# Second taps of the fourth group and their transfers ahead of the second group's result copies; fifth x, w2's sums and some scalings later; PSUM banks of one group dealt anew

## The chip, the core and the metric

The kernel runs on one core of a Trainium2 chip. A core has a matrix engine (TensorE, in the profile PE, with its weight loads as PEld), a vector engine (VectorE, DVE), a scalar engine (ScalarE, ACT), GpSimd (POOL), a sync engine that only issues transfers (SyncE, SP), and 16 DMA engines. Each engine works through its own list of instructions in order; semaphores tie the lists together. The metric is device time in microseconds (us) of one execution; less is better. The time before is 958.31 us, the median of three runs (956.83 to 960.3).

## The reference

Two blocks follow each other on x of 8 x 4224 x 192 in float32. First a causal convolution along the sequence, with 7 taps per head (8 heads of 24 columns), the taps softmaxed; then a layer norm without bias, an MLP 192 -> 768 -> 192 with relu, and a residual:

```python
w = softmax(weight)                       # [8, 7]
x_pad = concat([zeros(B, 6, D), x], 1)
y[b, s, h*24:(h+1)*24] = sum_k w[h, k] * x_pad[b, s + k, h*24:(h+1)*24]
mu, var = y.mean(-1), ((y - mu) ** 2).mean(-1)
yn = (y - mu) / sqrt(var + 1e-6) * g_ln
out = y + maximum(yn @ w_ch1, 0) @ w_ch2
```

## The kernel before, in words

**Groups.** The sequence is cut into 18 groups, g = 0 to 17, counted from zero in the code ("the fourth group" is g = 3, "the fifth x" is `xg[4]`). A group holds up to 16 rows of 192 columns for each of 128 partitions; group 0 has 6, group 1 has 8, groups 2 to 16 have 16, group 17 has 10. For each group x is loaded (`load_x`), convolved to `y`, transposed in 32 x 32 blocks to `yt` (DVE), taken up through w1 to the hidden tile `room` with relu, and taken down through w2 to `ot`; at last y is in `out` (`store_y`), and `ot` times the row's 1/std is added there by an accumulating DMA (`add_to_out`). The mean is folded into w1 and relu lets 1/std be applied behind w2, which is why the scaling (`scale`, L937 on ACT) comes last. 1/std is worked out by `root`, a chain of 19 small POOL instructions in two parts (9 before its first `yield`, 10 after), for two groups at a time; `next(pending, None)` in `up_mixed` puts each part in its place in the program.

**The convolution** is dealt out: tap 0 on ACT (`first_tap`, L375, into y), tap 1 on ACT (`second_tap`, L383, into a tile `tb`), and for g > 2 `tb` is added to y by four accumulating DMAs issued by POOL (`add_in_parts`, L408). Taps 2 to 6 are DVE instructions (`conv`, L416), one for each tap and head. For group 2 the third tap is on ACT too.

**Stages.** Groups 0 and 1 go through w1 and w2 by plain products (`up`, `down`). In `up(1)` six blocks f = 0..5 of 128 hidden columns are made, each into a set of four PSUM banks that ACT empties (L512); the two sets take turns, and `between` puts other ACT work behind an eviction. In `down(1)` PE makes two rows at a time into one bank (L799), ACT copies each bank out (L809), and second taps of group 3 stand behind the copies.
Groups 2 to 16 use a Strassen-Winograd scheme with seven products. `up_mixed(g)` does this in two passes, over hidden blocks 2 and 0..1 of each half (`one`, `two`), with two bank sets X and Y in turn: `evict` copies a set to SBUF on ACT (L637); `close` adds a set to an earlier partial result, either on DVE (L643) or by an ACT copy and an accumulating DMA issued by POOL (L601). Some of those copies lie for a while in parts of the tile that pass `two` writes later: `two.c22[:, 0:1]` is the source of the transfer that closes `one.c21`, and pass `two` evicts into the same place.
`down_fast(g, work)` does w2 the same way (PE at L854, ACT copies at L860, DVE sums at L897), with six banks. `work` is a list of ACT jobs (relus, scalings of the group before, first and second taps of group g + 2) that are put behind the copies, three, two, two and three behind each product's column blocks. Sums of w1's and w2's quarters (`w1sums`, `w2sums`, L573 on POOL) are made once, in group 1.

**What sets the order.** The order is written by hand: each engine runs its instructions in the order of the program text, and each wait holds all that is behind it on that engine. POOL's list holds its arithmetic and the issues of all accumulating transfers; SP's list holds the loads of x and the stores of y. Banks come from `take_bank` (one after the other, mod 8) and `take_set` (the next aligned four). `take_set` in `up_mixed` gives X, then Y; in `up_last`, for the last group, it gives Y, then X, while X is used first in both.

**Names and lines that matter here.** `between` L535-542; `up_mixed` L603-727 with `act_scales` L657 (two calls, L691 and L697), `store_y(g, nc.gpsimd)` L690, `work` L724-727; `down` L801-813; `down_fast` L835-913 with the bank deal L845-847; the main loop L1015-1078 with `load_x(g + 2)` L1018, `fourth_sum()` L1057, w2's sums L1058-1061, `pending = root(0)` L1062. The line `if g + 2 < NG and g != 1: load_x(g + 2)` loads x4 at the top of group 2. A load with `gate=True` puts a one-element DVE memset into the tile first, so that the transfer waits for that memset's place in DVE's list.

Of the kernel before, what the change touches and what calls it, by code (L numbers as in the profile page):

```python
# [16 lines left out]
def kernel(  # L17
# [29 lines left out]
    nc = tc.nc  # L47
    PSUM = bass.MemoryType.PSUM
    B, S, D = x.shape
    H, K = weight.shape  # L50
# [315 lines left out]
    def first_tap(g, heads=(0, H)):  # L366
        n = groups[g][2]
        if g == 1:

            y[g] = y[0][:, groups[0][2] :]  # L370
        elif heads[0] == 0:
            y[g] = ypool.tile([P, J, D], F32, tag="y", name=f"y{g}")
        for h in range(*heads):
            cs = slice(h * GRP, h * GRP + GRP)
            nc.scalar.mul(y[g][:, 0:n, cs], xg[g][:, 0:n, cs], taps[:, h, 0:1])  # L375
# [9 lines left out]
    def second_tap(g, heads=(0, H)):  # L385

        if heads[0] == 0 and g == 2:
            tb[g] = room[:, NF * J * Q :][:, 0 : J * D].rearrange("p (j d) -> p j d", d=D)
        elif heads[0] == 0:
            tb[g] = bpool.tile([P, J, D], F32, tag="tb", name=f"tb{g}")  # L390
        tap_products(g, tb[g], 1, heads)
        if g > 2 and heads[1] == H:
            add_in_parts(g, y[g], tb[g])
# [91 lines left out]
    def store_y(g, queue=nc.sync):  # L485
        n = groups[g][2]
        for ps, rows in rows_of_out(g, 0, n):
            queue.dma_start(out=rows, in_=y[g][ps, 0:n].rearrange("p j d -> p (j d)"))
# [46 lines left out]

    def between(g, f):

        if g == 1 and f == 4:
            first_tap(3, heads=(0, 3))
        elif g == 1 and f == 5:  # L540
            first_tap(3, heads=(3, H))
            second_tap(3, heads=(0, 2))

    def up(g):

# [57 lines left out]
    def up_mixed(g, ahead, pending):  # L603
# [53 lines left out]
        def act_scales(j1, j2):  # L657
            scale(before, j1, j2)
# [27 lines left out]
        p.product(X, a12, p.b21)  # L686
        for f in range(PAIR):
            p.close(p.c11[:, f : f + 1], X, rooms[0][:, f : f + 1], f)
        if g == 2:
            store_y(g, nc.gpsimd)  # L690
        act_scales(0, 1)  # L691
        p.product(Y, s2, p.t[0], False, False)
        p.evict(Y, p.c21)
        one.relu(one.c11)
        p.product(X, s3, p.t[1], True, False)
        p.evict(X, p.c22)
        act_scales(1, 2)  # L697
        p.product(Y, s1, p.b12, False, False)
        conv(g + 1, 2, 5)
        conv(g + 1, 5, 6, heads=(0, H // 2))  # L700
        p.close(p.c22, Y, rooms[1][:, 0:PAIR])
        p.product(X, a22, p.t[2], False)
        for f in range(PAIR):
            p.relu(p.c11[:, f : f + 1])
        lower_sum(g, (PAIR,))
        conv(g + 1, 5, 6, heads=(H // 2, H - 1))
        p.close(p.c21, X)
        p.product(Y, s4, p.b22, False)
        p.evict(Y, p.c12, True)
# [12 lines left out]
                    add_to_out(k, mid, n)  # L722

        work = [lambda: one.relu(one.c22)]  # L724
        work += [lambda j=j: scale_one(j) for j in range(2, done)]
        half = [lambda i=i: two.relu(two.c22[:, i : i + 1]) for i in range(PAIR)]
        return work[0:7] + [half[0], lambda: None, half[1]] + work[7:]

# [72 lines left out]
    def down(g):  # L801


        ot = out_tile(g)
        for j in range(0, groups[g][2], 2):
            bank = take_bank()[:, 0 : 2 * D].rearrange("p (j d) -> p j d", d=D)
            for i in range(2):
                down_row(bank[:, i], lambda f: ht[g][:, f, j + i].rearrange("p q t -> p (q t)"))
            nc.scalar.copy(ot[:, j : j + 2, :], bank)  # L809
            if g == 0 and j:  # L810
                third_tap(2, (0, 4) if j == 2 else (4, H))
            elif g == 1 and j < 6:
                second_tap(3, heads=[(2, 4), (4, 6), (6, H)][j // 2])

    def quarters_of_w2():
        return [
# [18 lines left out]
    def down_fast(g, work):  # L835
        n = fast[g]
        t = width(g)
        w = n * T
        a = of_products(g)
        flat = cpool.tile([P, NC, NFAST * C], F32, tag="cs", name=f"cs{g}")[:, :, 0 : n * C]  # L840
        halves = "p c (h j t) -> p c h j t" if t == C else "p c (j h t) -> p c h j t"
        cs = flat.rearrange(halves, h=2, t=t)
        free = a[:, 1, 0].rearrange("p f q j t -> p (f q) j t")
        parts = [free[:, 0:CH], free[:, CH : 2 * CH]]
        banks = [take_bank() for c in range(CH) for i in range(2)]  # L845
        if g + 1 == NG:
            banks = [banks[CH * i + c] for c in range(CH) for i in range(2)]

        def product(bank, left, right, to, first, behind=0):
            for c in range(CH):  # L850
                dst = banks[2 * c + bank]
                for f in (PAIR, *range(PAIR)):
                    for q in range(NQ):
                        nc.tensor.matmul(  # L854
                            dst[C * q : C * q + C, 0:w], right[:, f, C * c : C * c + C],
                            left[:, f, q], start=(first and f == PAIR), stop=(f == PAIR - 1),
                            skip_group_check=True,
                        )
                if to is not None:
                    nc.scalar.copy(  # L860
                        to[:, c], dst[:, 0:w].rearrange("p (j t) -> p j t", t=t)
                    )
                for one in work[:behind]:
                    one()
                del work[:behind]

        b = quarters_of_w2()
        c11, c21 = cs[:, 0:CH, 0], cs[:, 0:CH, 1]
        c12, c22 = cs[:, CH:NC, 0], cs[:, CH:NC, 1]
        if g + 2 < NG:  # L870
            work += [
                lambda tap=tap, h=h: tap(g + 2, heads=(h, h + 1))
                for tap in (first_tap, second_tap) for h in range(H)
            ]
        behind = (3, 2, 2, 3) if g + 1 < NG else (0, 0, 1, 1)
        product(0, a[:, 0, 0], b[0], c11, True, behind[0])
        product(1, a[:, 1, 0], w2sums[:, 2], c22, True, behind[1])
        product(1, a[:, 1, 1], w2sums[:, 3], c21, False, behind[2])
        product(1, a[:, 0, 1], b[2], None, True, behind[3])
        if g + 1 < NG:  # L880
            transpose(g + 1)
        inner, upper, right = a[:, 1, 1], a[:, 0, 0], a[:, 0, 1]
        if g + 1 == NG:
            size = FC * NQ * w
            other = bpool.tile([P, J, D], F32, tag="tb", name="sums").rearrange("p j d -> p (j d)")
            inner, upper, right = [
                v.rearrange("p (f q j t) -> p f q j t", f=FC, q=NQ, t=t)
                for v in (other[:, 0:size], other[:, size : 2 * size], room[:, 0:size])
            ]
        order = (PAIR, *range(PAIR)) if g + 1 == NG else range(FC)  # L890
        for dst, left, right_of, op in (
            (inner, a[:, 1, 1], a[:, 1, 0], ALU.add),
            (upper, inner, a[:, 0, 0], ALU.add),
            (right, a[:, 0, 1], inner, ALU.subtract),
        ):
            for f in order:
                nc.vector.tensor_tensor(dst[:, f], left[:, f], right_of[:, f], op=op)  # L897
        for c in range(CH):
            nc.vector.tensor_tensor(
                c11[:, c], c11[:, c], banks[2 * c + 1][:, 0:w].rearrange("p (j t) -> p j t", t=t),  # L900
                op=ALU.add,
            )
        product(0, inner, w2sums[:, 1], parts[0], False, 2)
        product(0, upper, w2sums[:, 0], parts[1], False, 2)
        for one in work:
            one()
        product(0, right, b[3], c12, False)
        if g + 1 < NG:
            sums_of_y(g + 1, nc.gpsimd)()
            moments(g + 1)  # L910
        else:
            finish_fast(g, 0, flat, cs, parts)
        return flat, cs, parts
# [100 lines left out]
    b11, b12, b21, b22 = quarters_of_w2()  # L1014
    for g in range(NG):  # L1015
        last = g + 1 == NG
        if g + 2 < NG and g != 1:
            load_x(g + 2)  # L1018
        if g < 2:
            up(g)  # L1020
# [25 lines left out]
        if g == 1:  # L1046
            conv(2, 3)
            flat = [v.rearrange("p j d -> p (j d)") for v in (y[2], tb[2])]
            nc.vector.tensor_tensor(flat[0], *flat, op=ALU.add)
            let_in(w1sums[:, 2])  # L1050
            sums_of_quarters(w1sums[:, 2], w21, w1sums[:, 0])
            transpose(2)
            fourth_sum = sums_of_y(2, nc.gpsimd)
            nc.vector.tensor_tensor(w12, w12, w11, op=ALU.subtract)
            moments(2)
            down(g)
            fourth_sum()  # L1057
            sums_of_quarters(w2sums[:, 2], b12, b22)  # L1058
            sums_of_quarters(w2sums[:, 0], b12, b11)
            sums_of_quarters(w2sums[:, 1], b22, w2sums[:, 0])  # L1060
            sums_of_quarters(w2sums[:, 3], b21, w2sums[:, 1])
            pending = root(0)  # L1062
            continue
        if g + 2 < NG:
# [44 lines left out]
```

## Time and profile before

| what | us |
|---|---|
| time of the profiled execution | 958.28 |
| its span, first to last instruction | 956.4 |
| median of three runs | 958.31 |
| PE busy | 940.8 |
| DVE busy | 892.3 |
| ACT busy | 716.6 |
| POOL busy | 340.6 |

The granted TensorE clock is 0.999. PE is idle for some 15 us in all, and these idle stretches are few. The groups in the middle are alike: PE takes 27.61 us for `up_mixed` and 27.33 us for `down_fast` in most of them. Group 2 does not: its `up_mixed` runs from 80.22 to 113.51 (33.29 us) and its `down_fast` from 113.51 to 141.57 (28.06 us). Group 16's `down_fast` runs from 885.18 to 913.08 (27.90 us). In a timeline each row has the start and length in us, then engine, line, operation, what it writes and reads, the count, and in brackets the engine's idle time just before it and what ended it.

### The profile page before, as it was taken

The numbers are of one execution on the slowest core, as the hardware profiler recorded it, in microseconds if no ns is written. First come the engines' busy times: TensorE is split into PE (matmuls) and PEld (weight loads), VectorE is DVE, ScalarE is ACT, GpSimd is POOL, SyncE is SP. The second block draws the span as 40 slices with busy tenths as digits, with TensorE's granted clock in tenths as the row PEclk, the third lists the DMA queues.
The fourth block names the chain that finished last, engine by engine and source line by source line (L and its number), as shares of the span: only waits on it lengthen the run. The fifth ranks groups of instructions, "written<-read, shape, count | busy, mean of one in ns | idle before, by whom it ended". The sixth has DMA issues, their size and how long they took to land. (4 is left out here: it accounts for less than half of the span.)

```text
span 956.4 us, 38496 instructions
## 1 busy us (share of the span) xinstructions
PE 940.8 (98%) x17106; PEld 742.7 (78%) x17106; DVE 892.3 (93%) x1479; ACT 716.6 (75%) x1275; POOL 340.6 (36%) x463
## 2 busy tenths in 40 slices
PE   9999799999999999999999999999999999999997
PEld 7999659687786979677686968778696877869586
DVE  8996999999999999999999999999999999997885
ACT  7865678969687796968778795978789596867543
POOL 2037455141533227141443217231451415332140
PEclk9999999999999999999999999999999999999999
DMA  8396896988979797897978887896979889676631
GB/s 208 122 196 170 202 270 121 252 161 188 217 131 277 133 252 151 216 204 136 263 144 239 169 226 156 175 249 135 265 137 245 163 181 202 127 171 124 101 64 49
DMA packets 38347, 171.94 MB, mean 180 GB/s; under 512 B 4517, under 2 KB 5798, under 8 KB 32039
## 3 DMA queue, kind: packets, MB, share of 16 engines
q0 software_dynamic: 31488, 106.87, 60.3%
q1 hardware_dynamic: 6688, 62.61, 18.1%
q8 instruction: 134, 2.20, 0.9%
q14 instruction: 31, 0.25, 0.1%
q10 hardware_dynamic: 6, 0.00, 0.0%
HBM read 38.92 MB, written 50.92 MB: 94 GB/s over the span
## 5 line engine op out<-in xcount | busy, mean ns | idle before, releaser
L416 DVE SCALAR_TENSOR_TENSOR y<-xg,taps,y 128x384 f32<-128x384 f32 (+3 forms) x710 | 358.8, 580 | 11.3 <-issue 9.7
L854 PE MATMUL ps<-room,w2sums 128*32 128x256 f32 (+1 forms) x4464 | 244.1, 376 | 1.3 <-issue 1.3
L637 ACT COPY room<-ps 128x512 f32<-128x512 f32 (+1 forms) x225 | 180.5, 844 | 64.8 <-PE ps L522 61.9
L522 PE MATMUL ps<-yt,w 32*128 32x256 f32 (+3 forms) x4092 | 226.3, 365 | 1.6 <-ACT room L512 1.0
L854 PEld LDWEIGHTS ps<-room,w2sums 128*32 128x32 f32 x4464 | 146.4, 110 | 93.1 <-issue 2.4
L522 PEld LDWEIGHTS ps<-yt,w 32*128 32x128 f32 x4092 | 203.2, 185 | 19.6 <-issue 7.2
L854 PE MATMUL ps<-room,w 128*32 128x256 f32 (+1 forms) x3456 | 191.0, 373 | 1.7 <-DVE room L643 1.2
L897 DVE TENSOR_TENSOR room<-room 128x1024 f32<-128x1024 f32 x135 | 154.6, 1218 | 16.8 <-PE ps L854 14.0
L854 PEld LDWEIGHTS ps<-room,w 128*32 128x32 f32 x3456 | 111.6, 110 | 72.8 <-DVE room L643 6.4
L522 PE MATMUL ps<-ysums,w1sums 32*128 32x256 f32 (+1 forms) x2304 | 132.2, 371 | 0.0
L522 PEld LDWEIGHTS ps<-ysums,w1sums 32*128 32x128 f32 x2304 | 121.3, 185 | 5.3 <-issue 0.2
L948 POOL DMA_DIRECT2D out_dram<-ot x70 | 59.9, 986 | 180.5 <-ACT ot L937 175.2
L860 ACT COPY cs<-ps 128x256 f32<-128x256 f32 (+1 forms) x192 | 70.6, 368 | 47.5 <-PE ps L854 47.1
L937 ACT ACTIVATE ot<-ot,r 128x192 f32<-128x192 f32 x238 | 100.8, 467 | 3.3 <-POOL r L482 3.3
L650 ACT ACTIVATE room<-room 128x1024 f32<-128x1024 f32 x90 | 94.9, 1064 | 4.2 <-DMA room<-parts_cs 2.7
L408 POOL DMA_DIRECT2D y<-tb x59 | 52.1, 1376 | 105.1 <-ACT room L860 98.2
L375 ACT ACTIVATE y<-xg,taps 128x384 f32<-128x384 f32 (+3 forms) x141 | 72.7, 608 | 2.2 <-DMA xg<-in_x_dram 1.3
L522 PE MATMUL ps<-yt,w1sums 32*128 32x256 f32 (+1 forms) x1152 | 71.6, 372 | 1.8 <-ACT room L637 1.8
L522 PE MATMUL ps<-ysums,w 32*128 32x256 f32 (+1 forms) x1152 | 71.1, 369 | 2.3 <-ACT room L637 2.3
L447 DVE BATCH_NORM_STATS2 st<-y 128x6 f32<-128x192 f32 x264 | 70.2, 346 | 0.0
L522 PEld LDWEIGHTS ps<-ysums,w 32*128 32x128 f32 x1152 | 62.6, 185 | 5.2 <-ACT room L637 2.7
L860 ACT COPY room<-ps 128x256 f32<-128x256 f32 (+1 forms) x96 | 35.6, 372 | 41.2 <-PE ps L854 40.6
(124 smaller groups left out, 959.6 us busy)
## 6 DMA issues: line engine op xcount, KB each, us to landing
xg<-in_x_dram SPq DMA_DIRECT2D x14, 2112.0 KB, 16.0
out_dram<-ot POOLq DMA_DIRECT2D x61, 384.0 KB, 9.5
room<-room POOLq DMA_DIRECT2D x45, 512.0 KB, 5.1
y<-tb POOLq DMA_DIRECT2D x58, 384.0 KB, 8.5
out_dram<-y SPq DMA_DIRECT2D x14, 1536.0 KB, 8.8
room<-parts_cs POOLq DMA_DIRECT2D x30, 512.0 KB, 6.8
room<-parts_tb POOLq DMA_DIRECT2D x15, 1024.0 KB, 7.6
xg<-in_x_dram SPq DMA_DIRECT2D x1, 1848.0 KB
```

The costliest lines, as they stand in the source:

```text
L375: nc.scalar.mul(y[g][:, 0:n, cs], xg[g][:, 0:n, cs], taps[:, h, 0:1])
L408: nc.gpsimd.dma_start(out=ends[0], in_=ends[1], accum_op=ALU.add)
L416: nc.vector.scalar_tensor_tensor(out=y[g][:, 0:n, cs], in0=t[:, k : k + n, cs], scalar=taps[:, h, k : k + 1], in1=y[g][:, 0:n, cs], op0=AL ...
L447: nc.vector.bn_stats(out=sums[g][:, j, :], in_=y[g][:, j, :])
L522: nc.tensor.matmul(banks[:, q, i * w + j1 * t : i * w + j2 * t], right[rows, c, P * i : P * i + P], left[rows, j1:j2, c, :], start=start, ...
L637: nc.scalar.activation(to, of, AF.Relu) if relu else nc.scalar.copy(to, of)
L650: nc.scalar.activation(c, c, AF.Relu)
L854: nc.tensor.matmul(dst[C * q : C * q + C, 0:w], right[:, f, C * c : C * c + C], left[:, f, q], start=(first and f == PAIR), stop=(f == PAI ...
L860: nc.scalar.copy(to[:, c], dst[:, 0:w].rearrange("p (j t) -> p j t", t=t))
L897: nc.vector.tensor_tensor(dst[:, f], left[:, f], right_of[:, f], op=op)
L937: nc.scalar.mul(ots[g][:, j, :], ots[g][:, j, :], rstd[g][:, j : j + 1])
L948: nc.gpsimd.dma_start(out=rows[:, d0:d1], in_=src[:, d0:d1], accum_op=ALU.add)
```

## The change

- `between`: the first taps of group 3 stand behind the evictions of f = 3, 4 and 5 of group 1 (two, two and four heads) in place of f = 4 and 5, and all second taps of group 3, with their four accumulating transfers, stand behind f = 5; `down(1)` has none of them any more.
- `store_y(2, nc.gpsimd)` goes from the middle of `up_mixed(2)` to the place between `down(1)` and `fourth_sum()`.
- The four sums of w2's quarters go from behind `fourth_sum()` to `up_mixed(2)`, behind the transfer that closes `two.c22`. `root(0)` then comes right behind `fourth_sum()` in POOL's list.
- In group 2 `act_scales` is left out of `up_mixed`, and its two scalings stand at the front of the list `work` in `down_fast(2)`. The other groups are as before.
- `load_x(4)` goes from the top of group 2 to a late place in `up_mixed(2)`, with a gate on DVE.
- The six banks of `down_fast(16)` are dealt as those of `down_fast(17)` are: three in a row for the products that use `bank` 0, three for those of `bank` 1.

```diff
     def between(g, f):
 
-        if g == 1 and f == 4:
-            first_tap(3, heads=(0, 3))
-        elif g == 1 and f == 5:
-            first_tap(3, heads=(3, H))
-            second_tap(3, heads=(0, 2))
+        if g == 1 and f >= 3:
+            first_tap(3, heads=[(0, 2), (2, 4), (4, H)][f - 3])
+        if g == 1 and f == 5:
+            second_tap(3)
...
             p.close(p.c11[:, f : f + 1], X, rooms[0][:, f : f + 1], f)
-        if g == 2:
-            store_y(g, nc.gpsimd)
-        act_scales(0, 1)
+        if before:
+            act_scales(0, 1)
         p.product(Y, s2, p.t[0], False, False)
         p.evict(Y, p.c21)
         one.relu(one.c11)
         p.product(X, s3, p.t[1], True, False)
         p.evict(X, p.c22)
-        act_scales(1, 2)
+        if before:
+            act_scales(1, 2)
         p.product(Y, s1, p.b12, False, False)
         conv(g + 1, 2, 5)
         conv(g + 1, 5, 6, heads=(0, H // 2))
         p.close(p.c22, Y, rooms[1][:, 0:PAIR])
+        if g == 2:
+            sums_of_quarters(w2sums[:, 2], b12, b22)
+            sums_of_quarters(w2sums[:, 0], b12, b11)
+            sums_of_quarters(w2sums[:, 1], b22, w2sums[:, 0])
+            sums_of_quarters(w2sums[:, 3], b21, w2sums[:, 1])
         p.product(X, a22, p.t[2], False)
         for f in range(PAIR):
             p.relu(p.c11[:, f : f + 1])
         lower_sum(g, (PAIR,))
         conv(g + 1, 5, 6, heads=(H // 2, H - 1))
+        if g == 2:
+            load_x(g + 2, gate=True)
         p.close(p.c21, X)
...
-        work += [lambda j=j: scale_one(j) for j in range(2, done)]
+        work += [lambda j=j: scale_one(j) for j in range(2 if before else 0, done)]
...
             if g == 0 and j:
                 third_tap(2, (0, 4) if j == 2 else (4, H))
-            elif g == 1 and j < 6:
-                second_tap(3, heads=[(2, 4), (4, 6), (6, H)][j // 2])
...
         banks = [take_bank() for c in range(CH) for i in range(2)]
-        if g + 1 == NG:
+        if g + 2 >= NG:
             banks = [banks[CH * i + c] for c in range(CH) for i in range(2)]
...
-        if g + 2 < NG and g != 1:
+        if g + 2 < NG and g not in (1, 2):
             load_x(g + 2)
...
             moments(2)
             down(g)
+            store_y(2, nc.gpsimd)
             fourth_sum()
-            sums_of_quarters(w2sums[:, 2], b12, b22)
-            sums_of_quarters(w2sums[:, 0], b12, b11)
-            sums_of_quarters(w2sums[:, 1], b22, w2sums[:, 0])
-            sums_of_quarters(w2sums[:, 3], b21, w2sums[:, 1])
             pending = root(0)
             continue
```

## The prediction

> **What bounds the kernel now.** First I read the page's totals, then PE by time, because PE is busy nearly all the time: whatever shortens the run has to remove one of PE's few idle stretches, and whatever lengthens it has to make a new one.
>
> ```profile
> span 956.4 us, 38496 instructions
> PE 940.8 (98%) x17106; PEld 742.7 (78%) x17106; DVE 892.3 (93%) x1479; ACT 716.6 (75%) x1275; POOL 340.6 (36%) x463
> ```
>
> Some 15 us of PE idle are all there is to win. PE's timeline shows where a part of them lies: in group 2.
>
> ```profile
> 66.04 14.24 PE L799 MATMUL ps<-w,room 128*128 128x192 f32 x86 [0.23 <-ACT room L512]
> 80.22 2.89 PE L522 MATMUL ps<-yt,w 32*128 32x128 f32 x52
> ...
> 102.44 2.87 PE L522 MATMUL ps<-ysums,w 32*128 32x256 f32 x48 [2.31 <-ACT room L637]
> 106.80 2.87 PE L522 MATMUL ps<-yt,w1sums 32*128 32x256 f32 x48 [1.50 <-ACT room L637]
> 109.50 2.77 PE L522 MATMUL ps<-yt,w 32*128 32x256 f32 x48
> 113.51 4.09 PE L854 MATMUL ps<-room,w 128*32 128x256 f32 x72 [1.25 <-DVE room L643]
> ...
> 121.79 4.31 PE L854 MATMUL ps<-room,w2sums 128*32 128x256 f32 x72 [0.30 <-issue]
> ```
>
> Three waits of 2.31, 1.50 and 1.25 us, the first two for ACT copies, the third for a DVE sum; up_mixed(2) takes 33.29 us where the later groups mostly take 27.61. ACT's and DVE's timelines tell why those were late:
>
> ```profile
> 100.18 0.45 ACT L937 ACTIVATE ot<-ot,r 128x192 f32<-128x192 f32 x1 [3.25 <-POOL r L482]
> 100.54 1.84 ACT L637 COPY room<-ps 128x2048 f32<-128x2048 f32 x1
> 102.28 1.06 ACT L650 ACTIVATE room<-room 128x1024 f32<-128x1024 f32 x1
> 104.88 1.86 ACT L637 COPY room<-ps 128x2048 f32<-128x2048 f32 x1 [1.54 <-DMA room<-room]
> ```
>
> ```profile
> 93.63 14.91 DVE L416 SCALAR_TENSOR_TENSOR y<-xg,taps,y 128x384 f32<-128x384 f32 x28 [9.07 <-issue]
> ```
>
> (1) The scaling of group 0 waits 3.25 us for 1/std from POOL, and the eviction at 100.54 stands behind it. (2) The eviction at 104.88 waits for the transfer out of the place it overwrites; POOL issued that at 100.08, right after the last root instruction. (3) DVE waits 9.07 us ahead of the fourth group's convolution, for the added second taps (issued 82.00 to 83.65, the last landed at 93.25). Its sum at 111.17 is therefore late. POOL's timeline joins (1) and (2): root(0) runs only from 91.17 to 100.14, since w2's sums stood ahead of it.
>
> ```profile
> 86.00 2.87 POOL L573 TENSOR_TENSOR w2sums<-w 128x288 f32<-128x288 f32 x2
> 88.94 1.67 POOL L573 TENSOR_TENSOR w2sums<-w,w2sums 128x288 f32<-128x288 f32 x2
> 90.56 0.87 POOL L601 DMA_DIRECT2D room<-room  x1
> ```
>
> **The change, part by part.** Times are of the profiled execution: span 956.4, its own time 958.28, within 0.03 of the median 958.31.
>
> *First taps behind f = 3: a loss.* ACT's timeline near 63 us:
>
> ```profile
> 58.94 1.02 ACT L512 ACTIVATE room<-ps 128x1024 f32<-128x1024 f32 x1 [1.56 <-PE ps L522]
> 61.47 1.02 ACT L512 ACTIVATE room<-ps 128x1024 f32<-128x1024 f32 x1 [1.51 <-PE ps L522]
> 63.46 1.62 ACT L375 ACTIVATE y<-xg,taps 128x384 f32<-128x384 f32 x3 [0.96 <-DVE y L416]
> 64.99 1.00 ACT L512 ACTIVATE room<-ps 128x1024 f32<-128x1024 f32 x1
> ```
>
> The first tap waits 0.96 us. The view names DVE, but ACT's wait ended at 63.18, and the only arrival beside it is the last of 16 of x3's load, at 63.16 (the 15 others had come by 61.36). With taps behind f = 3 (eviction over at 59.96), ACT stands until 63.46; two taps at 0.52 each, then the eviction of f = 4 at 64.5 to 65.5 (before 61.47 to 62.49), two taps, that of f = 5 at 66.4 to 67.45 (before 64.99 to 65.99). down(1) uses the set of f = 4 first, so PE stands from 63.9 to 65.5, does five matmuls (10 instructions, 1.89 us), and needs f = 5 at 67.47; before it went on at 66.04. Loss +1.43. Ends: about 0 if the last arrival is with the others, 2.4 if it is 1 us later. I take 1.43, since nothing ahead of 63 us changes.
>
> *Second taps and their transfers.* On ACT: four first taps and eight second taps behind 67.45 at 0.52 end near 73.7; the copies of down(1) (first bank ready near 70) wait until then, but its four pairs have four banks, and PE waits for none. POOL issues the four transfers from 73.8 (0.55 each) ahead of w1's sum (73.81 before, now 76.05 to 78.7) and of s3, which waits for DVE's memset of 79.05 anyway: cost 0. Landing took 11.25 us from first issue to last landing, so 85.05 in place of 93.25. DVE's moments end at 84.55, so the convolution starts some 8 us earlier and the 1.25 goes. 24 + 4 instructions then end near 100, and the sum at L643 is ready for PE as in later groups.
>
> *POOL.* s3 ends at 82.06, the y2 store issues from 82.0 (three next to each other at 100.69, 101.22, 101.76 cost 0.54 each; its own row lasts 1.54; I take 1.3), fourth_sum from 83.3 (84.22 before); PE needs it at 89.5. The transfer closing c11 then waits for ACT alone, as in group 3: 4.29 after the stage's start. Let S = 80.22 + 1.43 = 81.65 be that start. Root's first part has 9 instructions. With DVE idle they stood 0.29 apart (92.12 to 93.30); under the convolution 0.53 (95.45 to 99.69), and the convolution now runs beside all of them. So S+4.9, 9 x 0.53, a transfer issue 0.65, 10 x 0.53: the transfer that frees the buffer is issued at S+15.6, 14.66 in the later groups with a root. Those waited only when it landed later than S+20.2: landings at 20.41, 20.43 and 20.84 made stages of 27.82, 27.84 and 28.25. From issue to landing it took 4.64 to 6.17 us in such groups, 4.70 here: S+20.2 to 21.8, residual stall 0 to 1.6. I take 0.4 (nearest: 4.7 to 5). The stage is then 28.0 in place of 33.29: -5.28. Without act_scales ACT's eviction comes at S+17.4, as in later groups, and the 2.31 goes whole.
>
> *A rule against it, weighed.* The rows above put the convolution's price on root at 0.24 us for each of 19 instructions. The Trainium skill, "SBUF — State Buffer", section "Who interferes with whom", says that a DVE instruction with two SBUF inputs and a GpSimd instruction that reads SBUF exclude each other for whole instructions. Taken to the letter, each root instruction would wait out a convolution instruction and then run, near 0.74 apart (an estimate), root would end 4 us later, and the forecast would be 957.3; the row, 0.53, decides, and I use that alone.
>
> *w2's sums* (four, 4.56 us from 86.00 to 90.56) move behind the transfer closing c22 (S+24.7): ready by S+30, that is 111.7; the first is used at 113.6 (S+28.0+3.9), the last at 117.5. The result transfers behind them (L948) first stood at 117.39. Cost 0; without that cover up to 2.
>
> *y2's store* no longer sits in POOL's queue ahead of c22's transfer, which took 11.1 us (109.15 to 120.29; 7.6 median), so ACT's relu and PE at 121.79 came late. down_fast(2) lost 28.06 - 27.33 = 0.73; the two scalings that go there (0.45 each) make its list as long as a later group's. I take -0.60, ends 0 and -0.73.
>
> *x4's load.* The gate (0.06 us on DVE) stands behind lower_sum and three taps, S+24; issue at 105.7. x4's taps may start as late as 123.1 without PE waiting: the copy behind twelve of them (6.3 us) must be done when the next product starts, 20.2 into down_fast. Loads took 8.8 to 17.4 us: 114.5 to 123.1. Cost 0, end +1. On SP only y3's store and x5's load stand behind it, both waiting for DVE longer.
>
> *Banks of group 16.* up_last's first product uses the bank that down_fast(16)'s last copy empties:
>
> ```profile
> 912.65 0.37 ACT L860 COPY cs<-ps 128x256 f32<-128x256 f32 x1 [0.92 <-PE ps L854]
> 913.08 5.17 PE L522 MATMUL ps<-yt,w 32*128 32x160 f32 x144 [0.49 <-ACT cs L860]
> ```
>
> Dealt anew, that set holds banks whose last reader, DVE at 908.0, is long done. DVE waits for PE right behind (0.80 at 918.39), so the gain passes on: -0.50, ends 0 and -0.57 (27.90 - 27.33).
>
> Sum: +1.43 - 5.28 - 0.60 - 0.50 = -4.95; 958.28 - 4.95 = 953.3. Between groups 3 and 16 PE waits for almost nothing, so the shift reaches the end.
>
> **Rivals.** (a) *The buffer's transfer stays late* (0.15). At 0.56 between root instructions (group 15's pace) and 6.17 to land it comes at S+22.4, stall 2.2: 955.1; with x4 1 us late 956.1. For it: DVE's whole convolution beside root. Against it: 0.53 measured on this very root. (b) *y2's store delays the sums behind it* (0.08), the rival on the other side. It now goes into POOL's queue ahead of the transfers closing c11, c22 and c21. It took 14.3 us from 101.76 to 116.05; counted from 85.05 that is 99.4, and the three behind it at 1.8 each (the spacing of the four y3 additions) land c21 at 104.8, S+23.1: 955.8; at 4.6 each, 113.2, S+31.5, stall 11.3: 964.2. It decides from a landing at S+25.5 on. Against it: the transfer before it landed only at 109.95, so it had 6.1 us to itself, and 85.05 + 6.1 is before c22's issue. (c) *x4 comes late and ACT blocks* (0.07): a landing at 126 is 2.9 late: 956.2. For it: a load of 2112 KB now next to 2 MB of sums. (d) *Loss without gain* (0.05): the early part costs 1.43 and group 2's waits return elsewhere: 959.7. For it: PE's lists are tight. Against: three separate causes all move.
>
> **How the numbers follow.** Forecast 0.65, rivals as above. Likeliest case's own range: 951.9 (x3 early, no residual) to 955.4. The range reaches to rivals (a) and (c): 951.9 to 957.3. A measurement of this kernel can tell about 0.3%, 2.9 us, from no change: faster means under 955.4, slower over 961.2. Faster: 0.65 and half of (a), 0.72; slower: 0.08, from (b)'s upper end and (d) going further; the rest 0.20.
>
> **What would show it.** Right: PE standing about 1.6 us near 64 and starting group 2 near 81.7; DVE's convolution at 85; no L937 in up_mixed(2); the 2.31 and 1.25 gone, the 1.50 at most 0.5; group 3 starting near 137.3 (141.57 before); no wait at up_last. Wrong: PE waiting inside down_fast(2) for ACT, first taps of x4 after 123, the buffer's transfer landing more than 22 us into the stage.

## The result, and the profile after

The changed kernel takes 961.53 us (median of 20 runs, 958.62 to 970.23), the kernel before 958.39 us beside it (20 runs). The ratio is 1.0038 with a 95% interval of 1.0021 to 1.0055: slower, where 953.3 was forecast. The profiled execution took 960.42 us, its span 958.4. Two of the 20 runs took 970.2 us, with a granted clock of 0.992 and 0.993 where the others had 0.996 to 1.0; no profile shows one of them, and what happened there stays open.

PE is as busy as before (98%), and nearly all that changed lies in groups 1 and 2. PE's timeline of the changed kernel (start, length, engine, line, operation, tiles, count, and in brackets the idle time before and what ended it):

```profile
65.05 16.16 PE L805 MATMUL ps<-w,room 128*128 128x192 f32 x96 [0.42 <-ACT room L512]
81.14 2.88 PE L522 MATMUL ps<-yt,w 32*128 32x128 f32 x52
...
100.68 2.96 PE L522 MATMUL ps<-ysums,w 32*128 32x256 f32 x48
106.23 2.87 PE L522 MATMUL ps<-yt,w1sums 32*128 32x256 f32 x48 [2.59 <-ACT room L636]
108.92 2.77 PE L522 MATMUL ps<-yt,w 32*128 32x256 f32 x48
111.62 4.09 PE L858 MATMUL ps<-room,w 128*32 128x256 f32 x72
115.53 4.07 PE L858 MATMUL ps<-room,w2sums 128*32 128x256 f32 x72
123.63 6.47 PE L858 MATMUL ps<-room,w2sums 128*32 128x256 f32 x72 [4.03 <-issue]
129.91 4.07 PE L858 MATMUL ps<-room,w 128*32 128x256 f32 x72
```

Of the three waits in up_mixed(2), the first (2.31) and the third (1.25) are gone; the one in the middle has grown from 1.50 to 2.59. A new wait of 4.03 us stands in down_fast(2), and the product behind it runs slowly (6.47 us where 72 such matmuls take 4.07). The trace shows why it is slow: the granted TensorE clock is halved from 121.7 to 128.5. In these two stretches, one ahead of the wait and one behind it, the columns are the stretch, its length, the busy time and instruction count of PE, PEld, DVE, ACT and POOL, the granted clock, the busy share of the DMA engines, and GB/s:

```profile
111.60:119.60 8.00, 8.00 (x148) 4.58 (x144) 7.84 (x12) 5.70 (x11) 3.62 (x3) 1.00 1.00 258
123.60:128.50 4.90, 4.87 (x48) 2.68 (x52) 0.00 (x0) 4.10 (x11) 0.00 (x0) 0.50 1.02 423
```

In a later group the products of down_fast start 3.88 us apart. Here the third starts 8.10 us behind the second (4.22 more), and the fourth 6.28 us behind the third (2.40 more). So of the 6.62 us that down_fast(2) takes over 27.33, the wait makes 4.22 and the halved clock 2.40.

Stage by stage, read off the starts in PE's timeline:

| stage | before | after | change | forecast |
|---|---|---|---|---|
| start of group 2 | 80.22 | 81.14 | +0.92 | +1.43 |
| up_mixed(2) | 33.29 | 30.48 | -2.81 | -5.28 |
| down_fast(2) | 28.06 | 33.95 | +5.89 | -0.60 |
| groups 3 to 15, and up_mixed(16) | 743.61 | 742.83 | -0.78 | 0 |
| down_fast(16) | 27.90 | 27.33 | -0.57 | -0.50 |
| group 17 | 43.29 | 42.70 | -0.59 | 0 |

ACT's timeline names what the new wait was for:

```profile
62.97 1.12 ACT L375 ACTIVATE y<-xg,taps 128x384 f32<-128x384 f32 x2 [2.98 <-DVE y L416]
...
104.31 1.86 ACT L636 COPY room<-ps 128x2048 f32<-128x2048 f32 x1 [2.98 <-DMA room<-room]
...
122.21 1.06 ACT L649 ACTIVATE room<-room 128x1024 f32<-128x1024 f32 x1 [4.76 <-DMA room<-parts_tb]
123.18 0.35 ACT L864 COPY cs<-ps 128x256 f32<-128x256 f32 x1
```

In the kernel before the same relu waited too, but less:

```profile
120.38 1.06 ACT L650 ACTIVATE room<-room 128x1024 f32<-128x1024 f32 x1 [1.36 <-DMA room<-parts_tb]
```

The row at 122.21 is the relu of the first block of two.c22. It waits for the accumulating transfer out of `parts_tb` (1 MB, issued by POOL at 108.24), which landed at 121.85, 13.6 us later; in the kernel before it took 11.1, in a typical later group 7.6. Behind the relu in ACT's list stands the copy of the second product's first bank (123.18 to 123.53). PE's third product adds to that bank and starts at 123.63, 0.1 us behind the copy; in the kernel before it was 121.69 and 121.79. x4's load (2112 KB) was issued by SP at 107.23 and landed at 118.35, so the two were under way together. By that time x4 was no one's worry: its first tap starts at 129.49.

The middle wait comes from POOL and DVE. POOL's timeline, then DVE's:

```profile
73.27 3.52 POOL L408 DMA_DIRECT2D y<-tb  x4 [15.89 <-ACT tb L383]
75.45 4.00 POOL L572 TENSOR_TENSOR w1sums<-w,w1sums 128x1152 f32<-128x1152 f32 x1
81.37 2.85 POOL L596 TENSOR_TENSOR ysums<-yt 128x768 f32<-128x768 f32 x1 [1.92 <-DVE ysums L595]
...
98.37 0.88 POOL L600 DMA_DIRECT2D room<-room  x1
```

```profile
77.19 3.08 DVE L591 TENSOR_TENSOR ysums<-yt 128x768 f32<-128x768 f32 x1
...
86.62 14.90 DVE L416 SCALAR_TENSOR_TENSOR y<-xg,taps,y 128x384 f32<-128x384 f32 x28
```

POOL's third sum of w1 now starts behind the four transfer issues, at 75.45, and is still running when DVE starts its first sum of y2's quarters. That DVE instruction takes 3.08 us; in the kernel before, where POOL was done at 76.44, the same one took 0.96 us:

```profile
73.81 2.63 POOL L573 TENSOR_TENSOR w1sums<-w,w1sums 128x1152 f32<-128x1152 f32 x1 [16.46 <-DVE w1sums L570]
77.15 0.96 DVE L592 TENSOR_TENSOR ysums<-yt 128x768 f32<-128x768 f32 x1
```

DVE's next steps and POOL's s3 (81.37 in place of 79.21) follow late, and with them root(0) and the transfer that frees two.c22 (98.37).

### The profile page after: what moved, and what is told of

Same layout as the page of the kernel before. It is cut to its first block, busy times and chain, and to the rows that moved or that the text cites. A ratio compares the mean times of both kernels' runs of the same rounds, so it can differ in the third digit from the quotient of the medians.

```text
span 958.4 us, 38499 instructions
## 1 busy us (share of the span) xinstructions
PE 941.4 (98%) x17106; PEld 748.6 (78%) x17106; DVE 895.0 (93%) x1480; ACT 716.4 (75%) x1275; POOL 344.6 (36%) x463
## 5 line engine op out<-in xcount | busy, mean ns | idle before, releaser
L858 PEld LDWEIGHTS ps<-room,w2sums 128*32 128x32 f32 x4464 | 150.2, 111 | 95.7 <-issue 8.6
L522 PE MATMUL ps<-ysums,w 32*128 32x256 f32 (+1 forms) x1152 | 71.2, 369 | 0.0
L522 PEld LDWEIGHTS ps<-yt,w1sums 32*128 32x128 f32 x1152 | 61.5, 185 | 6.8 <-ACT room L636 4.0
```

What stands on the lines that cost most here:

```text
L522: nc.tensor.matmul(banks[:, q, i * w + j1 * t : i * w + j2 * t], right[rows, c, P * i : P * i + P], left[rows, j1:j2, c, :], start=start, ...
L858: nc.tensor.matmul(dst[C * q : C * q + C, 0:w], right[:, f, C * c : C * c + C], left[:, f, q], start=(first and f == PAIR), stop=(f == PAI ...
```

## The experiments

Two theories for the larger loss. **Theory 1**: x4's load, moved beside the transfer that closes c22, slows that transfer by taking its share of the DMA engines. **Theory 2**: the transfer is slow because of what stands around it in POOL's list (w2's sums, result additions), and the load is innocent. The kernel before was timed again beside each run; its medians lie between 958.3 and 959.1 us, so the ratios are compared rather than the times. The stages below are each read from one profiled execution.

**x4 loaded early again.** The change with one part undone:

```diff
-        if g == 2:
-            load_x(g + 2, gate=True)
...
-        if g + 2 < NG and g not in (1, 2):
+        if g + 2 < NG and g != 1:
             load_x(g + 2)
```

> The changed kernel with x4's load back at the top of group 2, all else as changed. Theory 1 (x4's load, issued at 107.2 us next to the 1 MB addition that closes c22 at 108.2, shares the DMA engines with it and stretches it from 7.6 to 13.6 us): the addition lands 7 to 9 us after issue, down_fast(2) falls from 33.95 to 27.4-28.0 us, the time to 954-956 us. Theory 2 (the addition is slow because of what stands around it in POOL's list, w2's sums right behind its issue and the result additions): it still takes 12-14 us, down_fast(2) stays at 33-34 us, the time at 961 us. Either way up_mixed(2) keeps a wait of 1.5 to 2.6 us for the transfer out of two.c22, and the y3 additions may land up to 3 us later, as x4's load now shares the engines with them.

Measured 956.21 us, ratio to the kernel before 0.9979 (0.9967 to 0.9991). The c22 transfer took 7.9 us (109.52 to 117.37), down_fast(2) 27.33 us. Theory 1 fits, theory 2 doesn't: w2's sums are still where the change put them. Over the c22 transfer the mean busy share of the DMA engines is 0.68 here (139 GB/s) and 1.00 in the changed kernel (262 GB/s), which is what sharing them would look like. The 2.56 us wait in up_mixed(2) is untouched:

```profile
107.51 2.87 PE L522 MATMUL ps<-yt,w1sums 32*128 32x256 f32 x48 [2.56 <-ACT room L636]
110.21 2.77 PE L522 MATMUL ps<-yt,w 32*128 32x256 f32 x48
112.91 4.09 PE L856 MATMUL ps<-room,w 128*32 128x256 f32 x72
116.82 7.95 PE L856 MATMUL ps<-room,w2sums 128*32 128x256 f32 x144
```

**The late load alone**, in the kernel before:

```diff
-        if g + 2 < NG and g != 1:
+        if g + 2 < NG and g not in (1, 2):
             load_x(g + 2)
...
         conv(g + 1, 5, 6, heads=(H // 2, H - 1))
+        if g == 2:
+            load_x(g + 2, gate=True)
```

> The kernel before with only x4's load moved to its late, gated place. Theory 1: it now runs beside the additions that close c11 and c22 and beside y2's store, so the c22 addition, 11.1 us from issue to landing before, takes 14 to 17 us, down_fast(2) goes from 28.06 to 31-35 us, the time from 958.4 to 961-965 us. Theory 2: no change in down_fast(2), 958-959 us.

Measured 965.41 us, ratio 1.0068 (1.0055 to 1.0081), just over the expected range. The c22 transfer, which has y2's store ahead of it here, took 14.7 us (111.12 to 125.84; 11.1 in the kernel before), down_fast(2) 33.20 us, with the same new wait ahead of the third product and again a halved clock behind it (128.27 to 131.68):

```profile
127.34 5.81 PE L856 MATMUL ps<-room,w2sums 128*32 128x256 f32 x72 [3.94 <-issue]
```

So the late load is enough by itself, and without it the loss is gone.

**Half of x4's rows late.** 11 of the 22 rows of each partition at the top of group 2, the other 11 at the late place:

```diff
-        if g + 2 < NG and g not in (1, 2):
-            load_x(g + 2)
+        if g + 2 < NG and g != 1:
+            load_x(g + 2, part=0 if g == 2 else None)
...
-            load_x(g + 2, gate=True)
+            load_x(g + 2, part=1)
```

> The changed kernel with half of x4's rows (1 MB) loaded at the top of group 2 and the other half at the late, gated place. If the bytes beside the c22 addition are what stretches it, the addition takes about half the extra time: 10-11 us from issue to landing (7.9 with no load beside it, 13.6 with all of it), and down_fast(2) is 28-30.5 us. If the mere presence of a load does it, it takes 13 us and more.

A single run took 956.06 us. The c22 transfer took 11.2 us (108.06 to 119.25), down_fast(2) 29.37 us. Between 7.9 without a load beside it and 13.6 with all of x4, and a little over the 10 to 11 expected: the bytes count, not the mere presence of a load. 1.7 of the 11.2 us is the wait for the last of the 16 arrivals; up to the 15th the three kernels took 7.0, 9.5 and 13.1 us.

**The taps alone**, in the kernel before (`between` and `down` as in the change, all else as before):

```diff
-        if g == 1 and f == 4:
-            first_tap(3, heads=(0, 3))
-        elif g == 1 and f == 5:
-            first_tap(3, heads=(3, H))
-            second_tap(3, heads=(0, 2))
+        if g == 1 and f >= 3:
+            first_tap(3, heads=[(0, 2), (2, 4), (4, H)][f - 3])
+        if g == 1 and f == 5:
+            second_tap(3)
```

> The kernel before with only the taps of group 3 moved (first taps behind f = 3, 4, 5; all second taps and their additions behind f = 5). Expected from the trace of the change: ACT stands behind f = 3 for x3, group 2 starts 0.9 to 1.4 us later; the y3 additions land near 84-86 us; DVE's convolution starts some 6-8 us earlier, so the 1.25 us wait for DVE at the end of up_mixed(2) goes, while the waits for 1/std and for the two.c22 transfer stay or get longer, as root now runs under the convolution. POOL's third sum of w1, now behind the additions' issues, stands against DVE's first sum of y2's quarters, which takes 3 us in place of 0.96. Time 957.5 to 960.5 us. If instead the taps alone explain the loss of the whole change, it is over 961 us.

Measured 961.11 us, ratio 1.0026 (1.0016 to 1.0036), just over the expected range and just inside the other branch (over 961). The time alone can't refute that branch; the kernel with x4 early does, which has the same taps and is faster than the kernel before. The profiled execution, 959.60 us, is the fastest of nine. As expected the 1.25 us at the end of up_mixed(2) is gone and the two others stay:

```profile
104.45 2.87 PE L522 MATMUL ps<-ysums,w 32*128 32x256 f32 x48 [2.66 <-ACT room L636]
108.83 2.87 PE L522 MATMUL ps<-yt,w1sums 32*128 32x256 f32 x48 [1.51 <-ACT room L636]
111.53 2.77 PE L522 MATMUL ps<-yt,w 32*128 32x256 f32 x48
114.22 4.09 PE L851 MATMUL ps<-room,w 128*32 128x256 f32 x72
...
123.61 4.31 PE L851 MATMUL ps<-room,w2sums 128*32 128x256 f32 x72 [1.41 <-issue]
```

The gain did not last: the c22 transfer, which here still has y2's store ahead of it, landed only at 122.11, 40.2 us into the group (40.1 in the kernel before), and the wait in down_fast(2) grew from 0.30 to 1.41. Group 1's two stages took 32.75 us in place of 32.04, and DVE's first sum of the quarters 2.73 us.

**The bank deal alone**, in the kernel before:

```diff
-        if g + 1 == NG:
+        if g + 2 >= NG:
             banks = [banks[CH * i + c] for c in range(CH) for i in range(2)]
```

> The kernel before with only the six banks of down_fast(16) dealt anew. Expected: the wait of 0.49 us ahead of up_last's first product goes, down_fast(16) falls from 27.90 to 27.33 us, the time by 0.4-0.6 us, which five rounds may just not tell from nothing. If the gain is lost in the tail: the stages are shorter but the last three together are as long as before.

Measured 957.64 us, ratio 0.9991 (0.9981 to 1.0000): no clear verdict from the times, but the stage fell to 27.33 us and PE starts the last group without a wait:

```profile
910.49 4.07 PE L854 MATMUL ps<-room,w 128*32 128x256 f32 x72
914.49 5.17 PE L522 MATMUL ps<-yt,w 32*128 32x160 f32 x144
```

The gain is not lost in the tail either: down_fast(16) and group 17 together took 70.6 us here, 70.0 to 70.9 in the other eight profiles with the new deal, and 71.2 to 71.8 in the three with the old one.

**y2's store back in up_mixed(2)**, x4 early:

```diff
             down(g)
-            store_y(2, nc.gpsimd)
             fourth_sum()
...
+        if g == 2:
+            store_y(g, nc.gpsimd)
         if before:
             act_scales(0, 1)
```

> The change with x4 loaded early and with y2's store back in the middle of up_mixed(2). Theory of the prediction: ahead of the c22 addition in POOL's transfer queue the store makes that addition land 11 us after issue in place of 7 to 9, and down_fast(2) takes 27.8-28.8 us in place of 27.33; the transfer out of two.c22 is issued 0.6 us earlier, as POOL does not issue the store ahead of root. Time within 0.5 us of 956.2 or up to 1 us over it. Rival: the store's place costs nothing, down_fast(2) stays at 27.33 us and the 0.6 us are won.

Measured 957.73 us, ratio 0.9992 (0.9981 to 1.0003), one thousandth above the ratio with the store moved; the two intervals overlap, so the times don't settle it. In the profiles both halves came as expected: the transfer out of two.c22 went 0.6 us earlier (16.6 us into the stage, 17.2 with the store ahead of root) and its wait was 2.07 us; the c22 transfer took 10.1 us and down_fast(2) 28.30. Moving the store was worth 0.97 us in down_fast(2) and cost 0.48 in up_mixed(2) (29.97 us with it back, 30.45 without).

**w1's third sum ahead of the y3 additions**, x4 early. The second taps stay in `between`, the four transfers go behind the sum:

```diff
-            second_tap(3)
+            second_tap(3, add=False)
...
             sums_of_quarters(w1sums[:, 2], w21, w1sums[:, 0])
+            add_in_parts(3, y[3], tb[3])
```

> The change with x4 loaded early, and with the four y3 additions issued behind POOL's third sum of w1 in place of ahead of it. Theory: that sum, pushed from 73.8 to 75.5 us by the issues, overlapped DVE's first sum of y2's quarters, which took 3 to 4 us in place of 0.96 and held up all behind it on DVE and POOL. Then the DVE sum is back at 0.96 us, s3 starts near 79-80 us, the transfer that frees two.c22 is issued at 15.6-16.3 us into the stage (17.2 in the change) and the wait for it falls from 2.56 to 0.5-1.6 us; time 0.8-1.8 us under that of the early-x4 kernel (956.2). Rival: the transfer itself takes 5.8 us in place of 4.7 because an instruction fetch of 16 KB falls on it, wherever it is issued; then the wait shrinks by less than 0.5 us.

Measured 954.69 us, ratio 0.9958 (0.9942 to 0.9973). The order on POOL is behind the 3 us: DVE's sum is back at 0.96.

```profile
77.40 0.96 DVE L591 TENSOR_TENSOR ysums<-yt 128x768 f32<-128x768 f32 x1
```

s3 started at 79.47 and the transfer out of two.c22 was issued 16.1 us into the stage, both as the theory said. But the wait fell only from 2.56 to 2.08, as the rival said: from issue to landing it took 6.47 us (5.82 with x4 early alone). up_mixed(2) took 29.98 us in place of 30.45, so the stage shows less of a gain than the ratios do, and the intervals of the two ratios overlap.

**First taps behind f = 4 and 5 again**, x4 early, with w1's sum in the change's order and then with the mend above:

```diff
-        if g == 1 and f >= 3:
-            first_tap(3, heads=[(0, 2), (2, 4), (4, H)][f - 3])
+        if g == 1 and f >= 4:
+            first_tap(3, heads=[(0, 3), (3, H)][f - 4])
```

> The change with x4 loaded early and the first taps of group 3 behind f = 4 and 5 again, but with the y3 additions still ahead of POOL's third sum of w1. It tells apart which of the two mends made the fastest kernel (951.4). If the order on POOL matters by itself: DVE's first sum of y2's quarters still takes 3 us or so, the transfer that frees two.c22 is issued 17 us or more into the stage, PE waits 1.5-3 us for it, time 953.5-955.5 us. If the f = 3 stand alone made the difference: no wait in up_mixed(2), 951-952 us.

Measured 955.53 us, ratio 0.9969 (0.9957 to 0.9982). DVE's sum took 2.31 us, the transfer was issued 17.7 us into the stage, and PE waited 2.93 us; the product behind that wait ran in part at half the clock (107.13 to 110.54) and took 4.56 us in place of 2.87. So the f = 3 stand is not what held up_mixed(2).

> The same, and the first taps of group 3 behind f = 4 and 5 as in the kernel before (three and five heads), so that ACT does not stand behind f = 3 for x3; the second taps stay behind f = 5. Expected: no wait of PE ahead of down(1) but the 0.2 us of before, group 2 starts 0.9-1.4 us earlier than with the taps behind f = 3; time 952.5-954.5 us, faster than both kernels. If the loss behind f = 3 is only moved (the second taps now end as late), the time is that of the run above.

Measured 951.36 us, ratio 0.9932 (0.9918 to 0.9946): faster than both kernels, and under the expected range. The two mends together give more than each alone (955.53 and 954.69), by the ratios 0.47% over x4 early alone, where the two singly add up to 0.31%; the intervals are too wide to call that excess shown by the times. PE's timeline shows no wait in up_mixed(2), which takes the 27.61 us of a later group:

```profile
66.41 14.24 PE L803 MATMUL ps<-w,room 128*128 128x192 f32 x86 [0.58 <-ACT room L512]
80.58 2.89 PE L522 MATMUL ps<-yt,w 32*128 32x128 f32 x52
...
100.13 2.95 PE L522 MATMUL ps<-ysums,w 32*128 32x256 f32 x48
102.72 2.95 PE L522 MATMUL ps<-yt,w1sums 32*128 32x256 f32 x48
105.31 2.95 PE L522 MATMUL ps<-yt,w 32*128 32x256 f32 x48
108.19 4.09 PE L856 MATMUL ps<-room,w 128*32 128x256 f32 x72
112.10 7.95 PE L856 MATMUL ps<-room,w2sums 128*32 128x256 f32 x144
```

POOL's timeline of this kernel shows a part of why: the stage starts earlier against DVE's convolution (80.58 and 87.23; 82.14 and 87.54 with w1's sum first alone), so root's first instructions run before it begins.

```profile
84.93 0.87 POOL L600 DMA_DIRECT2D room<-room  x1 [0.28 <-ACT room L636]
...
86.50 0.21 POOL L459 TENSOR_SCALAR v<-v 128x14 f32<-128x14 f32 x1
86.79 0.21 POOL L459 TENSOR_SCALAR d<-d 128x14 f32<-128x14 f32 x1
87.08 0.22 POOL L470 TENSOR_TENSOR v<-v,d 128x14 f32<-128x14 f32 x1
87.39 0.53 POOL L459 TENSOR_SCALAR r<-v 128x14 int32<-128x14 int32 x1
```

Root instructions stand 0.3 apart up to 87.39 and over 0.5 from there on. The transfer out of two.c22 was issued 14.7 us into the stage (95.28), where the later groups with a root have it, and landed 4.75 us on. With w1's sum first alone it was issued at 16.1 and landed 6.47 us on. So of the 3.1 us by which it comes earlier, 1.4 is the issue, which the rows explain, and 1.7 the landing, whose cause stays open (see the last section). The next run repeats both (14.4 and 4.81).

**The same with x4 late**, the change's place and gate, nothing else:

> The fastest kernel (951.4) with x4's load back at the change's late, gated place and nothing else. If the load next to the c22 addition costs by itself, with no other wait in the stage to hide or to add to it: the addition takes 12-14 us in place of 7.6, down_fast(2) 32.5-34 us in place of 27.33, time 956.5-958.5 us. If the late load only hurt together with the other delays of the change, down_fast(2) stays under 29 us and the time under 953 us.

Measured 959.93 us, ratio 1.0016 (1.0006 to 1.0026). The c22 transfer took 14.1 us (106.17 to 120.31), down_fast(2) 35.24 us in place of 27.33, and up_mixed(2) kept its 27.61:

```profile
112.98 4.07 PE L858 MATMUL ps<-room,w2sums 128*32 128x256 f32 x72
122.08 6.76 PE L858 MATMUL ps<-room,w2sums 128*32 128x256 f32 x72 [5.03 <-issue]
```

That is the price of the one move without any other wait to hide or add to it: 7.9 us, of which 5.2 is the later start of the third product and 2.7 its pace under the halved clock (120.71 to 127.54). It is more than expected, as the expectation had no term for the clock, and enough to turn the fastest kernel into one slower than the kernel before.

## Why the prediction was wrong

**x4's load, "Cost 0, end +1": the step that failed.** It asked only whether x4 would come in time for its own taps. It did, at 118.35 against a limit of 123.1. The step did not ask what else was on the DMA engines at 105 to 120 us: the 1 MB addition closing c22, on which ACT's relu, the copy behind it and PE's third product hang. That addition had landed 6.8 us into down_fast(2) in the kernel before, with PE waiting 0.30 already, so it had no slack. The term put at 0 measured 6.6 us in the changed kernel's stage (33.95 against 27.33 with x4 early), and 7.9 us where it stands alone (the last run). 2.4 and 2.7 us of these are the halved clock behind the wait, which the prediction had no term for. Rival (c) named the neighbours ("a load of 2112 KB now next to 2 MB of sums") and picked the wrong victim: it had the sums delay x4. All three of the prediction's signs of being wrong came: PE waiting inside down_fast(2), x4's first taps at 129.49, and the buffer's transfer landing 23.1 us into the stage. The first two name the stage of the miss, though its sum did not price it.

**The buffer's transfer, residual 0.4: mis-sized.** It was 2.59. The issue came 17.2 us into the stage, not 15.6: root began at 6.05, not 4.9, and took 0.5 longer with the issue between its parts. The step about w1's third sum, "cost 0", counted POOL's queue alone. Pushed behind the issues, that sum stood against a DVE instruction with two SBUF inputs, and 2.2 us of delay came back to POOL through the memset that s3 waits for. The forecast had weighed DVE holding up POOL and not POOL holding up DVE. The Trainium skill, "SBUF — State Buffer", section "Who interferes with whom", says that a DVE instruction with two SBUF inputs contends with a GpSimd instruction that reads SBUF, that the lock is exclusive, and that the order of issue decides which of the two blocks. This trace agrees: POOL's sum was first (75.45), and DVE's 3.08 us instruction ended at 80.27, 0.82 us behind the end of POOL's sum at 79.45. The row for root under the convolution held: 97.97 - 93.72 for eight steps is 0.53 each. Landing took 5.84 us where 4.7 was nearest, within the stated range of 4.64 to 6.17. Rival (a), a late transfer with a stall of 2.2, came close to what happened in this stage, but not for its reasons: it had root slower (0.56) and no later start of root.

**First taps behind f = 3, +1.43: right in kind, smaller here.** x3's last arrival was at 62.66 in this execution and ACT stood from 59.99 to 62.97; +0.92. In the runs with this part it was +0.7 to +2.1 over the 32.04 us of group 1's stages before, inside the stated 0 to 2.4. With the taps behind f = 4 and 5 again it was -0.3 to +0.4.

**What was right.** The 2.31 us went, as forecast; no run separates the two parts that should do this, act_scales left out and root no longer behind w2's sums. The 1.25 went with the earlier additions, as the run of the taps alone shows (the convolution started at 86.62 in place of 93.63; 85 was forecast). The banks gave -0.57 for a forecast of -0.50. y2's store no longer delaying the c22 transfer was right too, as its return shows (28.30 against 27.33 us), but the load took its place. Rival (b), the store delaying the sums behind it, did not decide: c11's transfer took 7.07 us (5.57 with the store back behind it) but landed at 93.64, c22's at 97.05, and the transfer out of two.c22 23.1 us into the stage, short of the 25.5 from which (b) decides; with the store back it was 22.6. w2's sums cost nothing: with x4 early, down_fast(2) takes 27.33 us with them where the change put them.

So the sum: +0.92 - 2.81 + 5.89 - 0.57 and the small remainders of the table give +2.06 in the profiled span, where -4.95 was forecast. 6.5 of the 7.0 us between them is down_fast(2), 2.5 is up_mixed(2), and the other lines give 2.0 back. The medians differ by more, 3.1 us; the profiled execution lies 1.1 us under its kernel's median. A slip in the prediction's own sum: its lower end, 951.9, is called "x3 early, no residual" but leaves the residual of 0.4 in; without it the end is 951.5.

## What to carry to other kernels

When a transfer is moved, price what it does to the transfers already there, not only whether it arrives in time: list every transfer under way in its new window, and which of them has the least slack. A move on one queue also changes which instructions of two engines meet; look at both sides of the pair. A wait of the matrix engine can cost more than its length: look at the granted clock behind it. When a change has six parts, a loss in one can hide gains in the others: here one part undone and two mended turned +0.4% into -0.7%.

## What the runs showed that was not expected

A 2 MB load of x started about when a 1 MB accumulating transfer did (1 us before to 2 us behind it) nearly doubled the smaller one: 13.6 us with all of the load beside it, 11.2 with half, 7.9 with none in the changed kernel, and 14.1 against 7.6 in the mended one. In the kernel before, where y2's store stands ahead of the smaller one, it was 14.7 against 11.1.

The granted TensorE clock fell to half inside group 2 in five of the twelve profiles, for 3.41 us at a time or twice that: behind or within PE waits of 2.26, 2.66, 2.93, 3.94, 4.03 and 5.03 us. Waits of 2.31, 2.56, 2.59 and (in another kernel) 2.66 us had no such fall, so the length of the wait alone does not decide it; what does was not tested.

The landing of the transfer out of two.c22 varied from 4.7 to 6.5 us, and nearly all of that lies in the last of its 16 arrivals. In the kernel before, 15 came by 104.75 and the last at 104.78; in the changed one 15 by 103.03 and the last at 104.21. In the trace's DMA records a fetch of 16 KB on the instruction queue (0.9 to 1.7 us long) falls into the transfer's window in eight of these kernels, and in six of them the last arrival is 0.5 to 1.8 us behind the 15th; in the four without one in the window it is 0.05 us or less behind. That the fetch is the cause was not tested, and two kernels with one had no such delay (0.05 and 0.12).
